# The first k piece loaded as fp32 by SyncE's and ScalarE's queues and cast on chip, in a linear-attention and squared-ReLU FFN kernel

## The chip, the cores and the metric

The kernel runs on one core of a Trainium2 chip. The metric is the device time of one execution in microseconds (us). The engines of the core are named as the profile names them: PE (TensorE, matrix multiplications) with PEld (its weight loads), DVE (VectorE), ACT (ScalarE), POOL (GpSimd) and SP (SyncE, which only issues transfers here). Transfers (DMAs) are issued by POOL, by SP and by ACT, each on its own queue.

## The reference

A linear attention with a learned feature map, followed by a feed-forward network on the concatenated heads. B = 8 batches, H = 8 heads, S = 576 positions, D = 64, 128 features before the sign is doubled; the FFN takes 4608 tokens of width 512 through 2048 hidden units.

```python
def phi(x):
    proj = np.einsum('bhsd,df->bhsf', x, w_phi)
    proj = proj - np.max(np.abs(proj), axis=-1, keepdims=True)
    return np.concatenate([np.exp(proj), np.exp(-proj)], axis=-1)
q_p, k_p = (phi(q), phi(k))
kv = np.einsum('bhsf,bhsd->bhfd', k_p, v)
z = np.sum(k_p, axis=2)
num = np.einsum('bhsf,bhfd->bhsd', q_p, kv)
den = np.einsum('bhsf,bhf->bhs', q_p, z)[..., None] + 1e-06
attn = num / den
x = attn.transpose(0, 2, 1, 3).reshape(B * S, H * D)
h = np.maximum(x @ w_in, 0.0)
out = h * h @ w_out
```

All inputs and the output are fp32 in memory. The kernel computes its matrix products on bf16 operands.

## The kernel before

Every step of the kernel is an `Op` of a plan: an engine, a function that emits its instructions, and the names that it reads and writes. `ORDER` is a fixed list in which the steps are emitted, and `pin` chains the instructions of each engine in that order, so each engine, the issuing queues included, works through its own list strictly in order. Waits between engines come from the names that steps share. `GATES` and `FILL` hold, by step number, extra waits for transfers and filler matmuls that are put in front of certain steps.

The kernel treats the batches one after the other; the FFN of one chunk of 512 tokens runs interleaved with the attention of the next batch. Only the start matters here. Batch 0 is loaded by POOL's queue, which converts fp32 to bf16 on the way: `load` (line 248) for k and v, `load_q` (line 267) for q. A "piece" of k or v is two heads with their first 512 positions, laid out as 128 partitions by 512 values; the tile `xk[0]` holds four such pieces and the last 64 positions of all heads ("s"). For batch 0, k is loaded as piece 0, piece 1, pieces 2 and 3 together, and the two halves of "s". POOL's list begins: piece 0 of k, piece 1 of k, the first half of q, the making of the identity matrix (`f_ident`), pieces 2 and 3 of k, "s", the second half of q, v, and so on, ending with the FFN's weights.

`w_phi` is loaded twice, into the two halves of the partitions, one half by SP's queue and one by ACT's (lines 223 to 226), and cast to bf16 by DVE in `f_wcast` (line 228).

What then happens to a piece of k in batch 0 (`kgroup_ops`, with `first` true):

- `pe_transposes` (line 322): four PE transposes of 128x128, reading `xk` and the identity (line 328), into one PSUM bank, and one copy of the result to `kT` by DVE or ACT (`copy`, line 195 for DVE, 197 for ACT);
- eight matmuls with `w_phi` into two PSUM banks, one for each half of the heads (line 381);
- for half 0, the maximum of the absolute values on DVE (line 388), before its exps; for half 1, the exps exp(x) and exp(-x) on ACT (line 397), before its maximum. The exps of half 0 come behind those of half 1.

For q in batch 0: PE transposes (line 328), a copy to `qT` by DVE (line 195), then the projections in both orientations (lines 507 and 549), a maximum on DVE (line 514) and exps on ACT (line 564). ACT's exps need a function table, which a table load of its own puts in place once, before the first activation.

Fillers (line 853) are matmuls on a tile of zeros (`warm`) which keep PE at work while it waits for the first data: 15 ahead of k's first transposes, and further ones between the steps of the first 27 us.

The order in which the loads of the start are recorded, and so numbered:

```python
load(k, xk, 0, "xk", prs=((0, 1),))
...
add("POOL", (0.45, 0.6), f_ident, r=["ident0"], w=["ident"], what="ident")
load(k, xk, 0, "xk", prs=((1, 2), (2, 4)), single=False)
load_q(0, jjs=(0,), single=False)
load(v, xv, 0, "xv", prs=((0, 4),))
load_q(0, jjs=(1,))
```

`of` (line 292) gives the names that a reader of `xk`, `xq` or `xv` waits for.

Of the kernel before, what the change touches and what calls it, by code (L numbers as in the profile page):

```python
# [111 lines left out]
def kernel(  # L112
# [10 lines left out]
    nc = tc.nc  # L123
# [30 lines left out]
    def sb(name, shape, dt=BF16):  # L154
        return pool.tile([P, *shape], dt, name=name)
# [7 lines left out]
    wphi2 = sb("wphi2", [Fd])  # L163
    ident = sb("ident", [P])
# [127 lines left out]
    def of(tag, b, us):  # L292
        if tag == "xq" and b >= 2:
            return [(tag, b % 2, "g", pr) for pr in range(4)] + [(tag, b % 2, "s", hi) for hi in range(2)]
        qs = [("xq", b % 2, u, a) for u in us if u != "s" for a in range(3)] if tag == "xq" else []
        return qs + [(tag, b % 2, u) for u in us if u != "s"] + [(tag, b % 2, "s", hi) for u in us if u == "s" for hi in range(2)]
# [510 lines left out]
    load(k, xk, 0, "xk", prs=((0, 1),))  # L807
# [197 lines left out]
```

## Time and profile before

| | us |
|---|---|
| median of 3 runs | 356.57 |
| lowest and highest run | 356.17 and 356.6 |
| the profiled execution | 356.65 |
| its span, from first to last instruction | 354.6 |

The granted PE clock is 1.00 in the whole span. A row of the instructions in order of time gives start and length in us, the engine, the line of the kernel, the operation, output<-input, and in brackets how long the engine had been idle before and what ended that wait. A row of the chain of waits gives start, length, and who held the chain. "POOLq", "SPq" and "ACTq" stand for the queue side of an engine: the issue of a transfer.

### The profile page before, as it was taken

How to read it: one execution, taken by the hardware profiler on the slowest of the kernel's cores; microseconds unless marked ns; L12 is line 12 of the kernel's file. 1: busy time of each engine (PE TensorE's matmuls, PEld its weight loads, DVE VectorE, ACT ScalarE, POOL GpSimd, SP SyncE). 2: the span in 40 equal slices, each digit the busy share in tenths (PEclk: the TensorE clock that was granted, in tenths of full speed). 3: DMA queues.
4: the chain of work that ended last, by engine and by line, in shares of the span. 5: the costliest groups of instructions: out<-in, count | busy, mean ns of one | idle time of the engine just before them, and what ended most of it. 6: DMA issues, size and time to landing. Idle time of an engine off the chain costs nothing.

```text
span 354.6 us, 8429 instructions
## 1 busy us (share of the span) xinstructions
PE 343.6 (97%) x3400; PEld 192.4 (54%) x3400; DVE 276.7 (78%) x525; ACT 227.0 (64%) x428; POOL 95.6 (27%) x143
## 2 busy tenths in 40 slices
PE   7889999999999999999999999999999999999995
PEld 4668976544654555455544644455555544444452
DVE  4998998899979988989778878799889736736210
ACT  4998987599779775795678577769686311340301
POOL 8834450296509500288000820000000000000000
PEclk9999999999999999999999999999999999999999
DMA  8999979999989987899454994700221211010105
GB/s 100 171 197 201 197 89 153 152 117 182 194 160 130 161 140 149 189 98 155 86 115 110 108 200 94 161 9 31 46 46 45 55 38 60 30 59 2 59 1 176
DMA packets 96101, 39.59 MB, mean 112 GB/s; under 512 B 64576, under 2 KB 91584, under 8 KB 96064
## 3 DMA queue, kind: packets, MB, share of 16 engines
q0 software_dynamic: 45216, 18.36, 45.3%
q1 hardware_dynamic: 50528, 20.42, 26.8%
q8 instruction: 26, 0.43, 0.5%
q10 hardware_dynamic: 320, 0.30, 0.3%
q14 instruction: 11, 0.09, 0.1%
HBM read 36.77 MB, written 9.44 MB: 130 GB/s over the span
## 4 chain that ended last, share of the span: by engine, by line
PE 76%; DVE 10%; ACT 7%; DMA 4%; issue 2%; SPq 0%; POOL 0%; DVEq 0%; ACTq 0%; POOLq 0%
PE psum L784 30%; PE psum L719 25%; PE psum L579 5%; PE psum L354 4%; PE psum L730 3%; PE psum L472 3%; DMA xq<-in_q_dram 3%; DVE va L442 3%; PE psum L549 2%; DVE mq L514 2%; DVE h L703 2%; ACT hr L694 1%; ACT kn L415 1%; ACT kp L415 1%; DMA out_dram<-ot 1%
## 5 line engine op out<-in xcount | busy, mean ns | idle before, releaser
L784 PE MATMUL psum<-wout,h 128*128 128x512 bf16 x560 | 133.6, 379 | 0.6 <-DVE ot L195 0.6
L719 PE MATMUL psum<-xT,win 128*128 128x512 bf16 x448 | 106.1, 379 | 0.0
L694 ACT ACTIVATE hr<-psum 128x512 bf16<-128x512 f32 x96 | 55.3, 596 | 46.7 <-PE psum L719 24.5
L784 PEld LDWEIGHTS <-h 128*128 128x128 bf16 x560 | 50.2, 98 | 55.0 <-issue 1.9
L719 PEld LDWEIGHTS <-win 128*128 128x128 bf16 x512 | 47.5, 98 | 53.6 <-issue 3.1
L703 DVE TENSOR_TENSOR h<-hr 128x512 bf16<-128x512 bf16 x144 | 56.3, 415 | 16.4 <-ACT hr L694 15.6
L564 ACT ACTIVATE qp<-psum 128x1024 bf16<-128x1024 f32 (+1 forms) x40 | 37.3, 938 | 23.7 <-PE psum L549 22.1
L514 DVE TENSOR_REDUCE mq<-psum 128x8 f32<-128x1024 f32 (+1 forms) x40 | 44.1, 1109 | 3.7 <-PE psum L354 2.9
L409 DVE TENSOR_REDUCE mk<-psum 128x8 f32<-128x1024 f32 (+1 forms) x35 | 38.1, 1109 | 3.5 <-PE psum L354 3.5
L415 ACT ACTIVATE kp<-psum 128x1024 bf16<-128x1024 f32 (+1 forms) x35 | 32.8, 938 | 10.9 <-DVE mk L409 10.6
L564 ACT ACTIVATE qn<-psum 128x1024 bf16<-128x1024 f32 (+1 forms) x40 | 37.4, 938 | 1.3 <-PE psum L579 1.0
L696 DVE TENSOR_SCALAR hr<-psum 128x512 bf16<-128x512 f32 x48 | 32.6, 685 | 6.7 <-PE psum L719 5.3
L253 POOL DMA_DIRECT2D xv<-in_v_dram x26 | 19.3, 754 | 50.5 <-DVE va L442 47.3
L415 ACT ACTIVATE kn<-psum 128x1024 bf16<-128x1024 f32 (+1 forms) x35 | 32.7, 935 | 0.0
L442 DVE TENSOR_TENSOR va<-xv,va 64x256 bf16<-64x256 bf16 (+2 forms) x68 | 30.4, 461 | 1.6 <-ACT va L434 0.8
L591 DVE TENSOR_TENSOR psum<-psum,en 128x520 f32<-128x520 f32 (+1 forms) x40 | 27.6, 698 | 3.9 <-PE psum L579 2.5
L197 ACT ACTIVATE ot<-psum 128x512 f32<-128x512 f32 x18 | 10.7, 594 | 27.1 <-PE psum L784 27.1
L603 DVE TENSOR_TENSOR xo<-psum,rden 128x512 bf16<-128x512 f32 (+1 forms) x40 | 27.3, 685 | 0.8
L253 POOL DMA_DIRECT2D xk<-in_k_dram x28 | 20.7, 746 | 11.5 <-ACT va L428 6.0
L195 DVE COPY ot<-psum 128x512 f32<-128x512 f32 x17 | 11.5, 684 | 15.1 <-PE psum L784 7.9
L472 PE MATMUL psum<-va,kp 128*128 128x65 bf16 x256 | 19.5, 193 | 0.8 <-DVE va L442 0.4
L273 POOL DMA_DIRECT2D xq<-in_q_dram x24 | 17.5, 733 | 10.3 <-ACT va L428 3.0
(68 smaller groups left out, 404.4 us busy)
## 6 DMA issues: line engine op xcount, KB each, us to landing
out_dram<-ot SPq DMA_DIRECT2D x32, 256.0 KB, 2.7
xk<-in_k_dram POOLq DMA_DIRECT2D x26, 128.0 KB, 4.3
xq<-in_q_dram POOLq DMA_DIRECT2D x24, 128.0 KB, 5.4
xv<-in_v_dram POOLq DMA_DIRECT2D x24, 128.0 KB, 4.3
win<-in_moe_w_in_dram POOLq DMA_DIRECT2D x4, 512.0 KB, 12.1
wout<-in_moe_w_out_dram POOLq DMA_DIRECT2D x4, 512.0 KB, 11.8
xq<-in_q_dram POOLq DMA_DIRECT2D x4, 256.0 KB, 6.1
xv<-in_v_dram POOLq DMA_DIRECT2D x2, 512.0 KB, 9.3
```

The costliest lines, as they stand in the source:

```text
L253: pin(nc.gpsimd.dma_start(out=x[:, a * 512 : z * 512].rearrange("p (h x) -> p h x", x=4 * D), in_=src[b][2 * a : 2 * z, 0:512, :].rearrang ...
L409: pin(nc.vector.tensor_reduce(out=mk_view(g), in_=ps2(pj)[:, :, : n * Fd].rearrange("p e (i f) -> p e i f", f=Fd), axis=AX.X, op=ALU.max, ...
L415: pin(nc.scalar.activation(out=dst[slot][:, :, :n, :].rearrange("p e i f -> p e (i f)"), in_=ps2(pj)[:, :, : n * Fd], func=ACT.Exp, scale= ...
L442: pin(engine().tensor_tensor(out=t[:, :, :D].rearrange("p m (x c) -> p m x c", c=2), in0=x.rearrange("p (m x c) -> p m x c", m=n, c=2), in ...
L472: pin(nc.tensor.matmul(out=o[:, sg, hi, :], lhsT=(kp, kn)[sg][kgroup[pr]][:, j % 2, 2 * hi + j // 2, :], rhs=va[s2][sg][:, 8 * pr + 4 * hi ...
L514: pin(nc.vector.tensor_reduce(out=mqb[:, c, :, :n], in_=ps2(pj)[:, :, : n * Fd].rearrange("p e (i f) -> p e i f", f=Fd), axis=AX.X, op=ALU ...
L564: pin(nc.scalar.activation(out=o, in_=i_, func=ACT.Exp, scale=sgn))
L694: pin(nc.scalar.activation(out=hr[sl], in_=ps1(g), func=ACT.Relu))
L696: pin(nc.vector.tensor_scalar(out=hr[sl], in0=ps1(g), scalar1=0.0, scalar2=None, op0=ALU.max))
L703: pin(engine().tensor_tensor(out=dst, in0=i_, in1=i_, op=ALU.mult))
L719: pin(nc.tensor.matmul(out=o, lhsT=win[mc // 4][:, kc, mc % 4 * P : (mc % 4 + 1) * P], rhs=x, start=(kc == 0), stop=(kc == KC - 1)))
L784: pin(nc.tensor.matmul(out=ps1(g), lhsT=h2[c % 2][mc // 4][:, mc % 4, tt * P : (tt + 1) * P], rhs=wout[mc // 4][:, mc % 4, :], start=(mc = ...
```

## The change

Piece 0 of k in batch 0 no longer goes through POOL's queue. A new tile `kf` (128 partitions by 512 values, fp32) takes it unconverted: partitions 0 to 63 by SP's queue, 64 to 127 by ACT's, each half 64 partitions of two runs of 1 KB. These two issues stand ahead of the two loads of `w_phi` on the same queues. Then ACT casts columns 0 to 255 to bf16 into `xk[0]`, and DVE columns 256 to 511; each cast waits for both halves. ACT's cast stands ahead of its first exp, DVE's ahead of `f_wcast`. The first two transposes of piece 0 read the columns that ACT casts, the other two those that DVE casts; `of` has a further name, `xk0`, so that the transposes wait for both. `load` for piece 0 now issues only the two "s" loads.

The plan has three steps more, so every number in `ORDER`, `GATES` and `FILL` from there on is three higher; apart from that and from the new steps, each engine has the same steps in the same order.

```diff
+    kf = sb("kf", [8 * D], F32)
...
+        qs += [("xk0",)] if (tag, b) == ("xk", 0) and 0 in us else []
...
-    load(k, xk, 0, "xk", prs=((0, 1),))
+    for hi, (name, e) in enumerate((("SP", nc.sync), ("ACT", nc.scalar))):
+        def fn(hi=hi, e=e):
+            pin(e.dma_start(
+                out=kf[hi * 64 : hi * 64 + 64, :].rearrange("p (h x) -> p h x", x=4 * D),
+                in_=k[0][0:2, hi * 256 : hi * 256 + 256, :].rearrange("h (p j) d -> p h (j d)", j=4)))
+        add(name, (0.6, 2.4), fn, w=[("kf", hi)], what="kf")
+    for half, (name, cost) in enumerate((("ACT", act_cost(256)), ("DVE", dve_cost(256)))):
+        def fn(half=half):
+            copy(xk[0][:, half * 256 : half * 256 + 256], kf[:, half * 256 : half * 256 + 256])
+        add(name, cost, fn, r=[("kf", 0), ("kf", 1)], w=[("xk", 0, 0) if half else ("xk0",)], what="kcast")
+    load(k, xk, 0, "xk", prs=())
```

More of the change, by code (lines that the diff above doesn't have):

```diff
@@ L959 @@
 GATES = {
[11 rows of a table removed]
[11 rows of a table added]
 }
 FILL = {
-    40: (0, 15, 0), 42: (0, 3, 0), 64: (0, 4, 0), 66: (0, 6, 0), 109: (0, 3, 0), 144: (0, 6, 0), 53: (0, 5, 0),
-    77: (3, 2, 0), 155: (7, 19, 0), 158: (7, 5, 0), 127: (2, 2, 0), 149: (6, 1, 0), 161: (6, 5, 0),
+    43: (0, 15, 0), 45: (0, 3, 0), 67: (0, 4, 0), 69: (0, 6, 0), 112: (0, 3, 0), 147: (0, 6, 0), 56: (0, 5, 0),
+    80: (3, 2, 0), 158: (7, 19, 0), 161: (7, 5, 0), 130: (2, 2, 0), 152: (6, 1, 0), 164: (6, 5, 0),
 }
```

192 rows, old and new, of tables (GATES, ORDER) are left out of this document.

## The prediction

> **What bounds the kernel now.** I read the page's first part, then the busy time by stage, then the chain of waits in order of time, then the instructions of the first 18 us one by one.
>
> ```profile
> span 354.6 us, 8429 instructions
> PE 343.6 (97%) x3400; PEld 192.4 (54%) x3400; DVE 276.7 (78%) x525; ACT 227.0 (64%) x428; POOL 95.6 (27%) x143
> ```
>
> TensorE is the bound over the whole, but an average says nothing about the first microseconds, which is all that this change touches. The stretches (columns: length, then busy time of PE, PEld, DVE, ACT, POOL, granted clock, DMA share, GB/s):
>
> ```profile
> 0.00:9.00 9.00, 6.74 (x58) 4.47 (x59) 3.82 (x11) 4.37 (x8) 7.90 (x15) 1.00 0.91 101
> 9.00:27.00 18.00, 15.80 (x253) 12.46 (x252) 17.55 (x38) 16.93 (x44) 10.28 (x16) 1.00 1.47 185
> 60.00:200.00 140.00, 138.77 (x1394) 73.30 (x1391) 123.74 (x221) 106.05 (x197) 59.51 (x88) 1.00 0.99 142
> ```
>
> Up to 9 us no engine is full: that is waiting. From 9 to 27 us VectorE is busy 17.55 of 18.00 us and ScalarE 16.93: both are nearly the bound there. After that TensorE is. What is won or lost before 9 us is therefore handed to VectorE and ScalarE, and from them to TensorE, with little room to swallow it. The chain, followed back from the end (start, length, what), begins like this:
>
> ```profile
> 0.64 0.61 issue
> 1.25 0.88 POOL xk L253 x2
> 2.12 0.63 issue
> 2.75 6.05 DMA xq<-in_q_dram
> 8.80 0.05 issue
> 8.85 0.41 PE psum L328 x4
> 9.26 0.02 issue
> 9.29 0.75 DVE qT L195 x2
> 10.04 1.20 DVE mk L388 x2
> 11.23 1.98 DVE mq L514 x2
> ```
>
> The start is set by the first q load, third in GpSimd's queue behind two k pieces. The first k piece itself is not on it. How close its own path is, the instructions show (start, length, engine, line; in brackets the idle time before):
>
> ```profile
> 0.74 0.58 ACTq L225 DMA_DIRECT2D wphi_f<-in_w_phi_dram  x1
> 1.06 3.28 PE L853 MATMUL psum<-warm 128*128 128x248 bf16 x15 [1.06 <-DVE warm L234]
> 1.25 1.53 POOL L253 DMA_DIRECT2D xk<-in_k_dram  x2 [0.80 <-POOLq L989]
> 1.34 1.28 ACT L397 ACT_TABLE_LOAD   x1 [1.34 <-PEq L989]
> 2.75 0.92 POOL L284 DMA_DIRECT2D xq<-in_q_dram  x1
> 3.01 0.71 DVE L229 CAST wphi<-wphi_f 128x128 bf16<-128x128 f32 x1 [1.65 <-DMA wphi_f<-in_w_phi_dram]
> 3.44 0.35 DVE L245 MEMSET va<- 128x264 uint32 x2
> 4.38 0.46 PE L328 MATMUL psum<-ident,xk 128*128 128x128 bf16 x4
> 4.88 0.42 DVE L195 COPY kT<-psum 128x512 bf16<-128x512 bf16 x1 [1.08 <-PE psum L328]
> 7.40 0.49 PE L853 MATMUL psum<-warm 128*128 128x248 bf16 x3
> 8.85 0.62 PE L328 MATMUL psum<-ident,xq 128*128 128x128 bf16 x8 [0.96 <-DMA xq<-in_q_dram]
> 8.92 1.13 ACT L397 ACTIVATE kn<-psum 128x512 bf16<-128x512 f32 x2
> 10.68 1.02 ACT L564 ACTIVATE qp<-psum 128x1024 bf16<-128x1024 f32 x1 [0.63 <-PE psum L549]
> 15.90 1.36 ACT L397 ACTIVATE kn<-psum 128x256 bf16<-128x256 f32 x3
> 16.47 1.63 DVE L388 TENSOR_REDUCE mk<-psum 128x2 f32<-128x256 f32 x3
> ```
>
> Three things to see. TensorE's 15 filler matmuls end at 1.06 + 3.28 = 4.34, and the k transposes follow at 4.38: were k there sooner, TensorE could not take it sooner. The k path then occupies TensorE to 7.40 + 0.49 = 7.89, 0.96 before the q transposes, and ScalarE with exps to 8.92 + 1.13 = 10.05, 0.63 before q's first exp at 10.68. So a k path later by D shifts TensorE's q work by D - 0.96 if q lands early, and ScalarE's by D - 0.63.
>
> **The change, part by part.**
>
> *GpSimd.* One xk issue goes, half of the 1.53, so everything behind it is issued 0.77 earlier, q at 1.98. Its 128 KB also leave GpSimd's queue. q then lands earlier by 0.77 at least (its issue time), and by twice that, 1.53, if the bytes ahead of it held it up as long as their issue did: at 7.3 to 8.0 instead of 8.80. Even 8.0 is before TensorE can turn to it if k's path is late at all, so q leaves the bound.
>
> *The two loads.* They are issued where w_phi was, at 0.74; w_phi follows 0.58 later on the same queues. No row shows these loads. Landings, in us from issue:
>
> ```profile
> wphi_f<-in_w_phi_dram ACTq DMA_DIRECT2D x1, 32.0 KB, 2.2
> out_dram<-ot SPq DMA_DIRECT2D x32, 256.0 KB, 2.7
> xk<-in_k_dram POOLq DMA_DIRECT2D x2, 128.0 KB, 3.2
> ```
>
> Both halves together are 256 KB on those queues. Bounds: 2.2 (w_phi, an eighth of it) and 3.2 (one k piece by GpSimd's queue). I take 2.7, the row with the same bytes: landed at 3.44 (2.94 to 3.94).
>
> *ScalarE's cast, and what stands in front of it.* Before, ScalarE's first activation came at 5.82, and its function table had been loaded from 1.34 to 2.62, in idle time. The built changed kernel's instruction order on ScalarE reads:
>
> ```
> 3 L198 LoadActFuncSet [waits DMAHW1_49]
> 4 L198 Activation xk_75<-kf 128x256 [waits DMAHW0_49]
> ```
>
> The cast needs two DMA semaphores; one wait stands as an instruction of its own, and the table load comes after it. So 1.28 us of hidden work moves behind the landing. The cast itself (128x256 fp32) is bounded by
>
> ```profile
> L397 ACT ACTIVATE kp<-psum 128x256 bf16<-128x256 f32 x2 | 0.8, 384 | 0.0
> ```
>
> at 0.38. Sum: 3.44 + 1.28 + 0.38 + 0.05 (the hand-over, as from 8.80 to 8.85) = 5.15 for the first transpose, against 4.38: D = 0.77, with bounds 0.27 and 1.27. Queued behind the load and cast on ScalarE are only k's exps, which wait for the transposes anyway.
>
> *VectorE's cast* of the other 256 columns, w_phi's cast and two memsets stand ahead of kT's copy. Row: w_phi's cast of only 128 columns took 0.71 and ended at 3.72, just when GpSimd's q issue (2.75 + 0.92 = 3.67) did, so I read about 0.5 of it as blocked. The new cast is bounded by 0.2 (that rest) and 0.95 (one whole issue in front); the w_phi cast behind it likewise. I take 0.7 each, the row nearest: 3.44 + 1.4 + 0.6 (memsets) = 5.4, ahead of kT's copy at 4.88 + 0.77 = 5.65: hidden, by 0.2. With both at the high end, 5.9 is 0.3 too late. [...]
>
> *Down to the end.* TensorE is free for q at 7.89 + 0.77 = 8.66, with q landed: 0.19 earlier than before. ScalarE ends k's exps at 10.82, 0.14 later than q's exp began. VectorE gets q 0.19 earlier, but its later k reduces of the second half wait for ScalarE (`maxes(1)` follows `exps(1)`): in the last two rows above, ScalarE's three exps end at 17.26, so the second of them at about 16.8 (half a microsecond per exp), and VectorE, 0.4 into its three, takes the matching reduce at about 16.85. Room there: under 0.1; I take 0.07. ScalarE is busy without a listed wait from 10.68 to there, so its lateness decides: D - 0.63 - 0.07 = +0.07 us. The lower end, D - 0.96, would be -0.19.
>
> Against the profiled execution's own time, 356.65 (span 354.6 and 2.05 around it), that is **356.7**. The profiled execution is 0.08 above the runs' median of 356.57. With D from 0.27 to 1.27 the shift runs from -0.45 to +0.57: this case's own range is 356.1 to 357.3.
>
> **The rivals.**
>
> *The load does its whole work: the table is in place before k lands.* Then k is cast at 3.44 + 0.38 = 3.82, the fillers' end at 4.34 rules, D is about 0, and q is the bound again at 8.0 or TensorE's 7.89: shift -0.7 to -0.85, about 355.9. For it: the table load had idle time from 1.34. Against: the instruction order puts it after a wait, and an engine's queue is in order.
>
> *ScalarE needs time after the table load.* Place: between load and cast. Before, 3.2 us of idle time follow the load, so the trace cannot show it.
>
> ```profile
> 5.82 1.29 ACT L397 ACTIVATE kp<-psum 128x512 bf16<-128x512 f32 x2 [3.19 <-PE psum L381]
> ```
>
> Bounds: 0, and a second stretch like the load itself, 1.28. With 1.28, D = 2.05 and the shift is 2.05 - 0.70 = +1.35: 358.0. It decides as soon as it is over about 0.65, when the shift passes 0.7. [...]
>
> *VectorE blocked by GpSimd.* GpSimd issues without a pause from 1.25 to about 9. If each of the two casts loses to more than one issue (0.8 and 0.65 twice behind q, in the changed order), kT's copy starts not at 5.65 but at 6.3 to 6.8: D on VectorE up to 1.9, shift +0.7 to +1.2, about 357.6. Against: the old cast got in at the first boundary.
>
> **How the numbers follow.** The forecast has 0.5; the table in place 0.14; ScalarE's pause 0.2; VectorE blocked 0.12; 0.04 for something else. A difference of 0.2%, 0.71 us, is about the least that a measurement of this kernel can tell from none. Faster by that: most of the first rival and a sliver of the rest, 0.15. Slower by that: the last two rivals, and the forecast's edge with a landing past 3.2 us, 0.36. Within: 0.49. The range reaches from the first rival to the pause: 355.8 to 358.2.
>
> **What would show it.** In the changed profile: the two loads land at 2.9 to 3.9; ACT_TABLE_LOAD starts with that landing, not at 1.3; the cast follows it at once (a gap of over a microsecond would be the pause); the k transposes start at 5.15, after a TensorE wait that was not there; the q transposes near 8.7 with no DMA wait; q's first exp near 10.8 with no wait in front; VectorE's two casts end before 5.4. A table load at 1.9, or k transposes at 4.4, would make the forecast wrong to the fast side; k transposes after 5.8 to the slow side. If all these hold and the time still moves by over 0.7, the fault is in the step that carries the first 17 us to the end unchanged.

## The result, and the profile after

The changed kernel takes 358.84 us in the median (9 runs, 357.09 to 359.15) against 356.57 before (9 runs): a ratio of 1.0052, 95% interval 1.0038 to 1.0065. It is slower by about 2 us: past the forecast's own range (to 357.3) and past the whole range (to 358.2). The profiled execution took 358.48, its span is 356.6.

The first instructions of the changed kernel in order of time (start, length, engine, line; in brackets the idle time before):

```profile
1.55 0.84 SPq L226 DMA_DIRECT2D wphi_f<-in_w_phi_dram  x1
2.07 0.92 POOL L285 DMA_DIRECT2D xq<-in_q_dram  x1
4.01 1.28 ACT L198 ACT_TABLE_LOAD   x1 [4.01 <-DMA kf<-in_k_dram]
4.03 0.29 DVE L196 CAST xk<-kf 128x256 bf16<-128x256 f32 x1 [2.68 <-DMA kf<-in_k_dram]
5.19 0.23 DVE L230 CAST wphi<-wphi_f 128x128 bf16<-128x128 f32 x1 [0.86 <-DMA wphi_f<-in_w_phi_dram]
5.30 0.42 ACT L198 ACTIVATE xk<-kf 128x256 bf16<-128x256 f32 x1
5.77 0.61 PE L330 MATMUL psum<-ident,xk 128*128 128x128 bf16 x4 [1.44 <-ACT xk L198]
6.18 0.83 PE L865 MATMUL psum<-warm 128*128 128x248 bf16 x3
10.15 0.49 PE L865 MATMUL psum<-warm 128*128 128x248 bf16 x3
10.47 0.61 PE L330 MATMUL psum<-ident,xq 128*128 128x128 bf16 x8
12.42 1.04 ACT L566 ACTIVATE qp<-psum 128x1024 bf16<-128x1024 f32 x1
```

The table load stands at 4.01, right behind k's landing, and the cast follows it at 5.30 without a pause. The k transposes start at 5.77, 1.39 later than before (4.38). That far the forecast's mechanism shows, with a larger delay. Then comes something that it does not have: after TensorE's wait of 1.44 the matmuls take much longer. Three fillers take 0.83 at 6.18; three took 0.49 in the kernel before at 7.40, and take 0.49 here again at 10.15. Called "slow" or "half rate" below: three fillers more add about 0.6 to a slow group (six take 1.45 in a later row) and 0.3 to a fast one (six take 0.80 at 10.92). Those last three ahead of q start at 10.15 instead of 7.40, 2.75 later: 1.39 of late start and 1.36 of slow matmuls. From their start to q's transposes it is 0.32 now (10.47). Before, TensorE would so have been free at 7.72 and took q at 8.85: 1.13 of the 2.75 falls into that room, and q's transposes start 1.62 late. q's first exp on ScalarE follows at 12.42 with no wait in front.

Landings (us from issue), of the changed kernel:

```profile
kf<-in_k_dram ACTq DMA_DIRECT2D x1, 128.0 KB, 2.7
kf<-in_k_dram SPq DMA_DIRECT2D x1, 128.0 KB, 3.2
wphi_f<-in_w_phi_dram SPq DMA_DIRECT2D x1, 32.0 KB, 3.5
xq<-in_q_dram POOLq DMA_DIRECT2D x1, 256.0 KB, 6.3
```

ScalarE's half of k takes the forecast's 2.7, SyncE's half 3.2. Each cast needs both. w_phi, behind k in the same queues, now takes 3.5 on SyncE's queue from an issue at 1.55 (2.1 from 0.74 before). q lands at 2.07 + 6.3 = 8.4, two microseconds before TensorE asks for it.

The chain of waits (start, length, what):

```profile
0.74 3.20 DMA kf<-in_k_dram
...
4.01 1.28 ACT L198
...
5.30 0.43 ACT xk L198
...
5.77 0.61 PE psum L330 x4
6.38 0.62 PE psum L865 x3
...
27.09 1.02 ACT qp L566
```

The q load is gone from the beginning of the chain. In its place stand SyncE's load of k, the table load, the cast, and then TensorE's fillers and k steps. ScalarE's exp of the last line started at 25.43 before: 1.66 late there, so what was late at q (1.62) is handed on. The profiled execution as a whole is 1.83 longer.

The clock that the profile shows as granted says nothing of the slow matmuls. The stretch of the first 9 us in the changed kernel (start and end, length, busy time of PE, PEld, DVE, ACT and POOL, granted clock, DMA share, GB/s) has a granted clock of 1.00, as before:

```profile
0.00:9.00 9.00, 6.50 (x40) 4.35 (x41) 3.04 (x11) 3.00 (x5) 7.58 (x15) 1.00 1.03 128
```

### The profile page after: what moved, and what is told of

Its sections match the earlier page's. It is cut to its first block, busy times and chain, and to the rows that moved or that the text cites. A ratio compares the mean times of both kernels' runs of the same rounds, so it can differ in the third digit from the quotient of the medians.

```text
span 356.6 us, 8404 instructions
## 1 busy us (share of the span) xinstructions
PE 342.7 (96%) x3367; PEld 193.5 (54%) x3400; DVE 277.1 (78%) x526; ACT 227.5 (64%) x429; POOL 94.9 (27%) x142
## 4 chain that ended last, share of the span: by engine, by line
PE 71%; DVE 12%; ACT 6%; DMA 5%; POOL 2%; issue 2%; SPq 1%; DVEq 0%; ACTq 0%
PE psum L786 27%; PE psum L721 24%; PE psum L581 4%; PE psum L356 4%; PE psum L732 3%; PE psum L474 3%; DVE va L444 3%; DMA out_dram<-ot 3%; DVE mq L516 2%; PE psum L551 2%; DVE h L705 2%; DVE mk L390 1%; DMA xk<-in_k_dram 1%; ACT qp L566 1%; PE psum L750 1%
## 5 line engine op out<-in xcount | busy, mean ns | idle before, releaser
L786 PE MATMUL psum<-wout,h 128*128 128x512 bf16 x527 | 128.4, 379 | 3.1 <-issue 1.3
```

Of the source, the lines that this page charges most:

```text
L786: pin(nc.tensor.matmul(out=ps1(g), lhsT=h2[c % 2][mc // 4][:, mc % 4, tt * P : (tt + 1) * P], rhs=wout[mc // 4][:, mc % 4, :], start=(mc = ...
```

## The experiments

Two theories stood against each other. One: TensorE, waiting 1.44 us for k, misses the point at which its matmuls go to full rate, and pays for that with about 1.3 us; the point depends on chance in time. The other: the loss is all in the late start, through the table load, and what looks slow on TensorE comes from elsewhere.

**The changed kernel again** (no edit).

> The changed kernel once more, for the spread of its runs and a second profile. If the clock's phase decides: two groups of times, near 357.3 (full rate reached before the wait at 4.34) and near 358.8 (half rate until about 9.4), and a profile of the first group shows the matmuls after the wait at full rate, the k steps 1.3 us shorter. If not: one group, and any profile shows half rate after the wait.

Measured: 358.03 (6 runs: 357.21, 357.32, 357.52, 358.53, 358.78, 359.46), ratio 1.0051 (1.0033 to 1.0070). With the nine runs above, six of fifteen lie at 357.1 to 357.6 and nine at 358.5 to 359.5; none lies between. So the median depends on how many runs fall into each group. The granted clock does not part them: its mean is 0.993 in three of the upper nine and 0.999 or 1.000 in the other six, 0.997 to 1.000 in the lower six. The profiled execution is the one of 357.21:

```profile
4.00 1.28 ACT L198 ACT_TABLE_LOAD   x1 [4.00 <-DMA kf<-in_k_dram]
5.27 0.94 POOL L285 DMA_DIRECT2D xq<-in_q_dram  x1
5.63 0.64 DVE L230 CAST wphi<-wphi_f 128x128 bf16<-128x128 f32 x1 [1.30 <-DMA wphi_f<-in_w_phi_dram]
5.77 0.40 PE L330 MATMUL psum<-ident,xk 128*128 128x128 bf16 x4 [1.43 <-ACT xk L198]
6.00 0.48 PE L865 MATMUL psum<-warm 128*128 128x248 bf16 x3
8.80 0.49 PE L865 MATMUL psum<-warm 128*128 128x248 bf16 x3
9.13 0.61 PE L330 MATMUL psum<-ident,xq 128*128 128x128 bf16 x8
```

The same table load, the same start of the transposes at 5.77, the same wait of 1.43: but the matmuls are at full rate at once (four transposes in 0.40, three fillers in 0.48), and q's transposes start at 9.13 instead of 10.47. The late start is in both profiled executions, one of each group of times; the slow matmuls are in that of the upper group alone. ScalarE's exp that started at 27.09 in the slow one starts at 25.98 here, 1.11 earlier, and the whole is 1.27 shorter (357.21 against 358.48): that is about what the slow matmuls cost, between two executions of one kernel.

The chain of waits of this execution does not begin with the table load, but with w_phi:

```profile
1.56 3.98 DMA wphi_f<-in_w_phi_dram
...
5.63 0.64 DVE wphi L230
...
6.42 0.29 DVE kT L196
```

w_phi lands at 5.54, its cast takes 0.64, and two memsets stand behind it on VectorE. In order of time kT's copy starts at 6.33, 0.16 behind the end of the transposes (6.17); in the execution of 358.48 it started 0.04 behind their end. So w_phi's path is here about 0.1 longer than the one through the table.

**More fillers ahead of k**, so that TensorE does not wait.

```diff
-    43: (0, 15, 0), ...
+    43: (0, 27, 0), ...
```

> The changed kernel with 27 instead of 15 filler matmuls ahead of k's first transposes, nothing else. Theory 1 (TensorE stays slow after the wait): TensorE waits from 4.34 to 5.77 in the changed profile and its matmuls are at half rate until about 9.4; with fillers through the wait the full rate is reached near 4.5 as before, the k steps take 3.4 us on TensorE instead of 4.7, q's transposes start near 9.1 instead of 10.47, and the time falls to the late start alone, 1.39 - 0.70 = 0.7 over before: about 357.3, and the runs lie close together. Rival (the half rate comes from the transfers or from anything but idleness): the matmuls after 5.77 stay slow and the time stays at 358.5 to 359.

Measured: 357.05 (11 runs, 356.52 to 357.75), ratio 1.0015 (1.0006 to 1.0023). Nothing is left of the upper group. Its instructions:

```profile
1.06 5.55 PE L865 MATMUL psum<-warm 128*128 128x248 bf16 x27 [1.06 <-DVE warm L235]
6.44 0.39 PE L330 MATMUL psum<-ident,xk 128*128 128x128 bf16 x4
9.39 0.49 PE L865 MATMUL psum<-warm 128*128 128x248 bf16 x3
```

The 27 fillers took 5.55, about 0.21 each, hardly less than the 15 before (0.22): here the full rate came only near 6.3, and the expectation's "near 4.5" was wrong for this execution. But from then on all is fast, though the transposes start even later (6.44), and the last fillers ahead of q start at 9.39 instead of 10.15. Added work made the kernel faster, by the two ratios 0.37% or 1.3 us. The transfers are the same, so it is the waiting that can lead to slow matmuls behind it. How much of the 1.3 us is theirs this pair does not show: in the profiled executions the exp that started at 27.09 without the fillers starts at 26.58 with them, 0.51 earlier, and the rest arose later (last section).

**The kernel before, with a wait put in**: 8 fillers instead of 15, loads untouched.

```diff
-    40: (0, 15, 0), ...
+    40: (0, 8, 0), ...
```

> The kernel before with 8 instead of 15 fillers ahead of k's first transposes, so TensorE is idle from about 2.7 to 4.38; loads and casts as before. Theory 1: the matmuls after 4.38 run at half rate for 3 to 4 us though nothing else changed; k's steps take up to 1.3 us longer, ScalarE's first exps end up to 1.0 later, and after its 0.63 to 0.70 of room 0.2 to 0.5 us are left: 356.8 to 357.1. Rival: matmuls at full rate from 4.6, time as before, 356.4 to 356.6.

Measured: 358.18 (6 runs, 357.79 to 358.94), ratio 1.0051 (1.0039 to 1.0063), more than expected. Leaving out seven matmuls on zeros costs as much as the whole change. The instructions:

```profile
1.06 1.83 PE L853 MATMUL psum<-warm 128*128 128x248 bf16 x8 [1.06 <-DVE warm L234]
4.55 0.61 PE L328 MATMUL psum<-ident,xk 128*128 128x128 bf16 x4 [1.65 <-DMA xk<-in_k_dram]
4.95 0.83 PE L853 MATMUL psum<-warm 128*128 128x248 bf16 x3
9.04 0.61 PE L328 MATMUL psum<-ident,xq 128*128 128x128 bf16 x8
```

The matmuls after the wait are slow with no new load, cast or table wait in the kernel. In this execution, the shortest of the six (357.79), q starts only 0.19 late, and the exp that started at 25.43 before starts 0.21 late, at the lower end of what was expected; of the rest of the 1.14, 0.6 came at a store of the output that took 4.48 where it took 3.86 before (last section). How the six runs' median divides between slow matmuls and that store, the runs do not show; that the matmuls turn slow, they do.

**The table load early**: a tiny activation ahead of the cast, on the zero tile.

```diff
+            if half == 0:
+                pin(nc.scalar.activation(out=pre, in_=warm[:, :8], func=ACT.Copy))
             copy(xk[0][:, half * 256 : ...
```

> The changed kernel with a tiny activation (8 columns of the zero tile) ahead of ScalarE's cast, so that the function table is loaded before the wait for k. The load then runs from about 2.1 to 3.4 and the cast follows the landing: k's transposes start near 4.5 instead of 5.77. Theory 'the table is all': the loss goes, 356.2 to 356.6. Theory 'w_phi is late too': w_phi lands only at about 5.1, VectorE's cast of it and two memsets end near 6.0, so kT's copy starts at 6.0 instead of 4.88 and only 0.4 us of 6.42 is won; TensorE idles there and may stay slow: 357 to 358.

Measured: 357.2 (12 runs, 356.64 to 359.03), ratio 1.0027 (1.0014 to 1.0040): inside the range of the second theory. Its profiled execution (356.79):

```profile
2.15 1.28 ACT L819 ACT_TABLE_LOAD   x1 [2.15 <-issue]
4.15 0.42 ACT L199 ACTIVATE xk<-kf 128x256 bf16<-128x256 f32 x1 [0.50 <-DMA kf<-in_k_dram]
4.62 0.61 PE L331 MATMUL psum<-ident,xk 128*128 128x128 bf16 x4 [0.28 <-ACT xk L199]
5.03 0.53 PE L868 MATMUL psum<-warm 128*128 128x248 bf16 x3
5.10 0.27 DVE L231 CAST wphi<-wphi_f 128x128 bf16<-128x128 f32 x1 [0.64 <-DMA wphi_f<-in_w_phi_dram]
5.81 0.36 DVE L197 COPY kT<-psum 128x512 bf16<-128x512 bf16 x1
```

The transposes are back at 4.62, 1.15 sooner. kT's copy, which they feed, starts at 5.81 (4.88 before): w_phi's cast and two memsets stand in front of it on VectorE, and w_phi lands at 5.1. That is the second delay, which the first one all but covered. Three of the twelve runs are still at 358.6 to 359.0.

**The same, and the two memsets ahead of the wait** (only the order of VectorE's steps).

```diff
-    4, 3, 9, 10, 0, 1, 5, 16, 18, 11, 12, 2, 6, 15, 8, 17, ...
+    4, 3, 9, 10, 0, 1, 5, 6, 8, 16, 18, 11, 12, 2, 15, 17, ...
```

> As the run with the early table, and the two memsets that stood behind w_phi's cast on VectorE now stand ahead of the wait for k, in idle time. kT's copy then starts right after w_phi's cast, at about 5.45 (4.88 before), 0.55 late, within ScalarE's room of 0.63 to 0.70; q, which landed at 8.4 in the changed profile, starts at 8.45 instead of 8.85. If table and w_phi are all: 356.2 to 356.6, as before or a little under. If the half rate of TensorE also strikes: 357 to 357.5.

Measured: 356.88 (12 runs, 355.96 to 358.50), ratio 1.0016 (1.0004 to 1.0028). The median is 0.4 over before; two runs are at 358.2 and 358.5. One of these two is the profiled execution:

```profile
4.55 0.61 PE L331 MATMUL psum<-ident,xk 128*128 128x128 bf16 x4 [0.21 <-ACT xk L199]
4.95 0.83 PE L868 MATMUL psum<-warm 128*128 128x248 bf16 x3
5.49 0.42 DVE L197 COPY kT<-psum 128x512 bf16<-128x512 bf16 x1
7.73 1.45 PE L868 MATMUL psum<-warm 128*128 128x248 bf16 x6
10.24 0.65 PE L331 MATMUL psum<-ident,xq 128*128 128x128 bf16 x8
```

Everything is early (kT's copy at 5.49), yet six fillers take 1.45 at 7.73: TensorE waited 0.21 and, ahead of the projections, 0.18 us, and in this execution it stayed slow until about 10.2. That these short waits are the reason is not shown by this trace alone.

**Both casts on VectorE**, none on ScalarE, memsets early.

```diff
-    ... (("ACT", act_cost(256)), ("DVE", dve_cost(256)))):
+    ... (("DVE", dve_cost(256)), ("DVE", dve_cost(256)))):
```

> The changed kernel with both casts on VectorE (512 columns in two instructions) and the two memsets early; ScalarE casts nothing, so nothing holds its table load. If the load's 1.28 us behind the wait was the main cost: the load starts near 2.2, k's transposes near 4.7 instead of 5.77, the time is that of the early table with early memsets, 356.6 to 357.0, with some runs near 358.4. If ScalarE's table was not it: 358 and over.

Measured: 356.69 (12 runs, 356.24 to 358.34), ratio 1.0009 (1.0000 to 1.0018). Without the cast on ScalarE, nothing ties the table load to k's landing. The instructions of its profiled execution, the one run at 358.34:

```profile
2.15 1.28 ACT L399 ACT_TABLE_LOAD   x1 [2.15 <-issue]
4.26 0.56 DVE L196 CAST xk<-kf 128x256 bf16<-128x256 f32 x2 [2.33 <-DMA kf<-in_k_dram]
4.61 0.67 PE L330 MATMUL psum<-ident,xk 128*128 128x128 bf16 x4 [0.26 <-DVE xk L196]
```

Two casts on one engine end at 4.82, where one cast behind a table load ended at 5.72. The matmuls of this one execution are slow again (four transposes in 0.67); how they are in the other eleven runs, all under 357.4, no trace shows.

**Early table, early memsets, and the short waits filled.**

```diff
-    43: (0, 15, 0), 45: (0, 3, 0), ...
+    43: (0, 17, 0), 45: (0, 5, 0), ...
```

> The run with the early table and early memsets, with 17 instead of 15 and 5 instead of 3 fillers, so that TensorE's two waits of 0.2 and 0.2 to 0.4 are filled. If the clock follows how full a stretch of a few us was, with a phase that differs from run to run: the runs near 358.3 vanish and all lie at 356.0 to 357.2. If the slow runs have another cause: some remain over 358.

Measured: 356.62 (11 runs, 356.43 to 357.29), ratio 1.0008 (1.0000 to 1.0017). With four fillers more no run is over 357.3, about as the first theory expects (356.0 to 357.2). It is weak support: the version without them had two of twelve over 358, and if these two had fallen at random among the 23 runs, the eleven would have been free of them about one time in four. It is not faster than the kernel before: kT's copy starts at 5.87, since w_phi lands late.

**The four transfers sorted anew**: both halves of w_phi by SyncE, both halves of k by ScalarE, and w_phi's cast ahead of k's on VectorE, on top of the last version.

```diff
-    for half, (name, e) in enumerate((("SP", nc.sync), ("ACT", nc.scalar))):
+    for half, (name, e) in enumerate((("SP", nc.sync), ("SP", nc.sync))):
...
-    for hi, (name, e) in enumerate((("SP", nc.sync), ("ACT", nc.scalar))):
+    for hi, (name, e) in enumerate((("ACT", nc.scalar), ("ACT", nc.scalar))):
```

> The early table load and the early memsets, and the four small transfers sorted anew: both halves of w_phi on SyncE's queue, both halves of k's piece on ScalarE's, w_phi's cast ahead of k's on VectorE, 17 instead of 15 and 5 instead of 3 fillers in the two short waits. If w_phi's late landing (5.1) held kT's copy: w_phi lands near 3.5, k near 4.2, the transposes start near 4.7 and kT's copy near 5.2 (4.88 before, 5.49 with the early memsets alone), 0.3 late, and q's landing at 7.7 to 8.4 instead of 8.80 is worth up to 0.4: 356.0 to 356.5, the same as or just under the kernel before. If two transfers in one queue land one after the other and late (k at 5 or later): 356.8 to 357.5.

Measured: 359.2 (6 runs, 357.45 to 360.36), ratio 1.0073 (1.0051 to 1.0095), at least as bad as the change itself. The instructions:

```profile
0.74 1.49 ACTq L812 DMA_DIRECT2D kf<-in_k_dram  x2
4.79 0.23 DVE L231 CAST wphi<-wphi_f 128x128 bf16<-128x128 f32 x1 [2.87 <-DMA wphi_f<-in_w_phi_dram]
5.74 0.42 ACT L199 ACTIVATE xk<-kf 128x256 bf16<-128x256 f32 x1 [1.97 <-DMA kf<-in_k_dram]
```

k's second half, behind the first in one queue, is there only at 5.74, where halves on two queues were there at 4.0 to 4.4; and w_phi, both halves in a queue without k, is still cast only at 4.79. The miss was mine: I had taken the second transfer of a queue to follow the first by its issue time of 0.7. The rival held, with a larger price; in this execution the matmuls behind TensorE's wait of 1.45 are slow as well (four transposes in 0.61 at 6.21), which is part of it.

No version tried beats the kernel before.

## Why the prediction was wrong

*What held.* The first k piece was not on the chain; GpSimd's issues moved 0.7 up (q from 2.75 to 2.07) and that was worth nothing, as k's path became the bound. q itself landed at 8.4 in one execution and at 7.5 in the other, where 7.3 to 8.0 was forecast, both times before TensorE asked for it. The table load moved behind the landing with its 1.28. The step "D - 0.63 - 0.07" also held, for one execution: with D = 1.39 it gives 0.69, and the execution of 357.21, without slow matmuls, is 0.56 over the profiled execution before (356.65). ScalarE did bind there, from 7.91 to 14.64 without a break on that execution's chain. And in the change's two profiled executions what was late at 25 us was late at the end within 0.2 (1.66 and 1.83; 25.98 against 25.43, 0.55, and 0.56). In two of the experiments it was not: 1.15 became 0.40 with 27 fillers, 0.21 became 1.14 in the kernel before with 8.

*What failed, first: the term for the landing.* I took 2.7 from the row of a 256 KB store, and the slower of two concurrent halves took 3.2, my upper end. With 0.07 to the table load and 0.43 for the cast, D is 1.39 instead of 0.77: of the sum, 0.6 us. This alone would have left the time near 357.3, at the edge of the forecast's own range, and there the lower group of runs lies. (A slip in the range itself, without effect: with D = 0.27 the sum's own step gives -0.43, not -0.45.)

*What failed, second, and put the time out of the range: the sentence that the k path "shifts" TensorE's q work by D - 0.96.* It took TensorE's matmuls to be as long as before. From the first k transposes to the last fillers ahead of q it was 3.02 us before and 3.03 in the execution of 357.21, but 4.38 in that of 358.48: 1.36 us that the sum had put at nothing. I had read the 15 fillers only as something that ends at 4.34 and so bounds the gain; I did not ask what they are for, nor what a gap behind them does. I named no rival with this mechanism. The traces show it from both sides: with 27 fillers the slow stretch behind the k transposes is gone, with 8 in the kernel before it appears. What it costs is read best from the two executions of the changed kernel (1.11 by 27 us, 1.27 in all), since the times of the other two carry the store of the last section. By the two groups of times nine of fifteen runs paid it and six did not, so that the median did was chance. The rows of before had the signs: the first 15 fillers took 3.28, 0.22 each, while three later ones took 0.49, 0.16 each.

*What failed, third: w_phi.* I let it follow k's issue by 0.58 with its old landing; it landed over 2 us later than before (5.1 and 5.5 in the two executions, instead of 2.9). In the execution of 358.48 this is hidden by the larger delay; in that of 357.21 the chain runs through it, by about 0.1; with the table early it is what holds kT's copy (5.81 and 5.49 against 4.88).

*The rivals.* The table in place before k lands: false for the change. When it is forced (early table, memsets early), the time is 0.4 over before, not 0.7 under: the gain that was to come from q is not there, as w_phi and k's path hold the rest. ScalarE's pause after the load: false, 4.01 + 1.28 = 5.29 and the cast starts at 5.30 (in the execution of 357.21 4.00 + 1.28 = 5.28, and again 5.30). The 1.28 that the prediction allowed for it was an estimate from the load's own length; the rows show 0.01 and 0.02. VectorE blocked by GpSimd: not the loss, but there in part. In the execution of 358.48 the new cast took 0.29 and w_phi's 0.23, where I had taken 0.7 each. In that of 357.21 w_phi's cast began at 5.63, 0.36 into GpSimd's q issue, took 0.64, and ended at 6.27, just behind that issue (5.27 + 0.94 = 6.21), as in the kernel before (3.72 and 3.67). The other traces divide the same way: w_phi's casts that began at most 0.22 into a q issue took 0.23 (early memsets, both casts on VectorE), and those that began 0.26 or more into it ended 0.05 to 0.06 behind its end. That fits a block for the rest of one issue, in no trace for two; it adds to the 0.1 above and does not explain the 2 us.

## What to carry to other kernels

Here the function's table was loaded right in front of the first activation, and when that activation waited for two transfers, the load waited with it: an early dependent activation moved 1.28 us of otherwise hidden work behind the landing, and a tiny activation on data at hand, or a cast on another engine, moved it back (the load started at 2.15 in both, instead of 4.01). When TensorE's start is delayed, reckon with matmuls at half rate behind the wait (here from 5.77 to about 9.4, in one of two profiled executions: three fillers took 0.83 instead of 0.48), and try filling the gap with idle matmuls: here 12 of them took the upper group of runs away. The load moved to the head of a queue delayed the one behind it by more than its issue time (w_phi was issued 0.8 later and landed over 2 later); follow each of them to its reader.

## What the runs showed that I had not expected

Whether the matmuls were slow was not the same in two executions of one kernel. The same instruction stream up to 10 us gave 9.13 and 10.47 for q's transposes. Nor is the point at which the matmuls reach full rate the same from trace to trace: near 6.3 with 27 fillers and no gap, near 5.1 with the early table and a wait of 0.28, and only near 10.2 with the early memsets and waits of 0.21 and 0.18. What sets that point no run measures: that it is how full a stretch of time was, as the expectation of the run with the short waits filled has it, was my guess. The profile's granted clock is 1.00 over the first 9 us in both executions all the same, so only the lengths of equal matmuls show it.

A second spread sits far from the change, at one output store. On the chain of waits of the kernel before it stands as

```profile
173.67 3.86 DMA out_dram<-ot
```

and on that of the kernel before with 8 fillers as

```profile
173.93 4.48 DMA out_dram<-ot
```

VectorE's next copy into that buffer waits for it. Here 0.26 of lateness became 0.88; with 27 fillers in the changed kernel, 1.15 became 0.4 at the same place. So up to 0.8 us comes and goes there, and the comparison of medians carries it too. What makes the store shorter or longer was not taken apart.
